# Linear attention beside a SwiGLU block on one core: a new order of work for the first five tiles

## The chip, the core and the metric

The kernel runs on one core of a Trainium2 chip. The core has five engines that work side by side and wait for each other through semaphores: TensorE (PE) multiplies matrices and writes to PSUM, ScalarE (ACT) evaluates functions, VectorE (DVE) does elementwise work and statistics, GpSimd (POOL) does elementwise work on SBUF, SyncE (SP) issues most DMAs. ACT issues some DMAs too. Every engine works its own queue strictly in the order in which it was written.

The metric is the device time of one execution in microseconds. The kernel before takes 211.72 us (median of three runs, 211.69 to 211.87). One further execution was profiled; it took 211.6 us, of which the profile's span covers 210.4.

## What is computed

The input x has 2048 rows of 512 in bfloat16. The output is the sum of three terms:

```python
xn = layernorm(x)                      # over the 512 columns, no scale or bias
q, k, v = xn @ wqkv                    # 32 heads of 16
phi = lambda t: where(t > 0, t + 1, exp(t)) + 1e-6
kv  = einsum("bhsd,bhse->bhde", phi(k), v)
z   = einsum("bhsd->bhd", phi(k))
o   = (phi(q) @ kv) / (phi(q) @ z + 1e-6)
out = x + o @ wo + (silu(x_ @ w_gate) * (x_ @ w_up)) @ w_down     # x_ is xn
```

The feature phi is built in the kernel as max(t, 0) + (min(exp(t), 1) + 1e-6).

## The kernel before

The 2048 rows are 16 tiles of 128. The kernel has two stages. In the first, for each tile, K and Q are projected (eight matmuls of 512 columns), phi(k) is formed, and the product of the normalized tile and phi(k) is accumulated over all tiles (`gtacc`, four matmuls, called GT below; it lives in the PSUM banks 4 to 7). In the second stage the SwiGLU block runs over four chunks of 512 rows, and the attention output and the projection back are added to it. The change lies in the first stage, and in its first five tiles above all.

No planner orders the work. The order is written out by hand: each call of a helper appends to the queue of one engine through `K.op(engine, function, r=reads, w=writes)`. `_Prog` keeps the last writer and the readers of each named resource and derives from them which semaphores an operation waits for. So the place of a call decides only its place in the queue of its own engine; the waits follow from the resources.

The steps that the change touches, with their engine and line:

- `bns` and `agg` (DVE, L296, L299): mean and variance of a tile. `rstd_pow` (L313): adds 1e-5 to the variance (L317, on POOL, for tiles 3 and 5 on DVE) and takes the power -0.5 (L324, always POOL).
- `xn_dve` (DVE, L304): the normalized tile, needs `rstd`. `xn(t)` is the same followed, from tile 3 on, by a DMA transpose on SP's queue (L377) that K and Q of the tile wait for.
- Tiles 0 to 2 take a shorter way: `xc_half` (DVE, L349) subtracts the mean, `tp_first` transposes on PE (L361) and copies on ACT (L370), `proj_first` (PE, L400) multiplies two of the four blocks of 128, and `rstd` is applied when ACT reads the result: `first_ek` (L457, exp of K), `first_pk` (L463, positive part of K), `first_eq` (L469, exp of Q), `first_pq` (L475, copy of Q).
- phi(k) of tile 0 is added on POOL (`feat_pool`, L482), of tiles 1 and 2 on DVE (`first_feat`, L489), after `clip` (DVE, L440) has cut the exponential.
- From tile 3 on: `kproj`, `qproj` (PE, L386), `exp_k` (ACT, L423), `exp_q` (ACT, L429 and the copy L433), `feat_k` (DVE: `clip` L440, `maxadd` L449, with the `zsum` of an earlier tile between them).
- `zsum` (POOL, L508 for tile 0, L512): adds phi(k) of a tile to the sum z. It is given the buffer of an exponential as a further read, so that it waits for the `clip` of a later tile.
- `fill` (PE, L268): matmuls on constants before the first data.

PSUM banks 0 to 3 hold K and Q of two tiles in turn: K of an even tile is in bank 0, Q in 1, K of an odd tile in 2, Q in 3. A projection thus waits until the readers of two tiles before are done. The loop over the tiles runs from tile 4. In step t it issues the projections and exponentials of tile t, the normalization of later tiles (`XN0`), the features of t, statistics of later tiles (`STAT`), and GT of tile t - 1 (from step 12 on of t - 2).

The queue of PE around the change runs: K 0, K 1, first halves of Q 0 and Q 1, second halves, K 2, GT 0, Q 2, GT 1, GT 2, K 3, Q 3, K 4, Q 4, GT 3, K 5, Q 5, GT 4 and so on. The queue of POOL runs: rstd 0 to 2, `feat_pool(0)`, rstd 3 to 7, zsum 0, rstd 8, zsum 1, rstd 9, zsum 2, rstd 10 and so on.

Of the kernel before, what the change touches and what calls it, by code (L numbers as in the profile page):

```python
# [6 lines left out]
ACT = mybir.ActivationFunctionType  # L7
# [101 lines left out]
def bass_parallel_sum__linear_attn_block__swiglu_ffn__prompt_kernel(  # L109
# [16 lines left out]
    with contextlib.ExitStack() as es:  # L126
# [120 lines left out]
        xload("sp", sp, 1, 1)  # L247
        wqkv_load("sp", sp, "wk", 1, 2, 1)
        wqkv_load("act", act, "wk", 1, 3, 1)
# [61 lines left out]
        VD = (3, 5)  # L311

        def rstd_pow(t):  # L313
            eng, h = ("dve", dve) if t in VD else ("pool", pool)
            K.op(
                eng,
                lambda: h.tensor_scalar(  # L317
                    out=vpe[:, t:t + 1], in0=mv[:, t, 1:2], scalar1=1e-5, scalar2=None, op0=ALU.add,
                ),
                r=[("mv", t)], w=[("vpe", t)],  # L320
            )
            K.op(
                "pool",
                lambda: pool.tensor_tensor(out=rstd[:, t:t + 1], in0=vpe[:, t:t + 1], in1=nhalf[:, :], op=ALU.pow),  # L324
                r=[("vpe", t), ("nhalf",)], w=[("rstd", t)],
            )
# [100 lines left out]
        def exp_q(t):  # L427
            K.op(
                "act", lambda: act.activation(eq[:, t, :], banks[qb(t)], ACT.Exp),  # L429
                r=[bk(qb(t))], w=[("eq", t)],  # L430
            )
            K.op(
                "act", lambda: act.activation(pkq[:, t, 1, :], banks[qb(t)], ACT.Copy),  # L433
                r=[bk(qb(t))], w=[("pq", t)],
            )
# [31 lines left out]
        def first_eq(t):  # L467
            K.op(
                "act", lambda: act.activation(eq[:, t, :], banks[qb(t)], ACT.Exp, scale=rstd[:, t:t + 1]),  # L469
                r=[bk(qb(t)), ("rstd", t)], w=[("eq", t)],  # L470
            )
# [20 lines left out]

        def feat_k(t):
            e = t % NE
            clip(ek[:, e, :], ("ek", e))
            if t >= 3:
                zsum(t - 3, e)
            maxadd(pkq[:, t, 0, :], banks[kb(t)], ek[:, e, :], [bk(kb(t)), ("ek", e)], [("pk", t)])
# [30 lines left out]
        def stat(t):  # L529
            bns(t)  # L530
            agg(t)
            rstd_pow(t)
# [6 lines left out]
        bns(0)  # L539
        agg(0)  # L540
        rstd_pow(0)
        xc_half(0, 0)
        xc_half(0, 1)
        bns(1)
        agg(1)
        rstd_pow(1)
        xc_half(1, 0)
        xc_half(1, 1)
        bns(2)
        agg(2)  # L550
        rstd_pow(2)
        xn_dve(0)
        xc_half(2, 0)
        xc_half(2, 1)

        fill(8, 512)
        tp_first(0, 0, 4)
        fill(2, P)
        tp_first(0, 1, 5)
        fill(3, P)  # L560
        proj_first(0, "wk", 0)
        tp_first(1, 0, 6)
        tp_first(1, 1, 7)
        proj_first(0, "wk", 1)
        first_ek(0)
        first_pk(0)
        proj_first(1, "wk", 0)
        proj_first(1, "wk", 1)
        first_ek(1)
        proj_first(0, "wq", 0)  # L570
        proj_first(1, "wq", 0)
        tp_first(2, 0, 4)
        tp_first(2, 1, 5)
        proj_first(0, "wq", 1)
        proj_first(1, "wq", 1)
        clip(ek[:, 0, :], ("ek", 0))
        feat_pool(0)
        bns(3)
        agg(3)
        rstd_pow(3)  # L580
        bns(4)
        clip(ek[:, 1, :], ("ek", 1))
        first_pk(1)
        first_eq(0)
        first_pq(0)
        proj_first(2, "wk", 0)
        proj_first(2, "wk", 1)
        gtacc(0)
        xn_dve(2)
        xn(3)  # L590
        agg(4)
        first_feat(1)
        rstd_pow(4)
        xn_dve(1)
        first_ek(2)
        first_pk(2)
        first_eq(1)
        first_pq(1)
        clip(ek[:, 2, :], ("ek", 2))
        xn(4)  # L600
        proj_first(2, "wq", 0)
        proj_first(2, "wq", 1)
        gtacc(1)
        first_eq(2)
        xload("act", act, 14, 2)
        first_pq(2)
        first_feat(2)
        bns(5)
        agg(5)
        rstd_pow(5)  # L610
        gtacc(2)
        bns(6)
        agg(6)
        rstd_pow(6)
        xn(5)
# [3 lines left out]
        exp_q(3)  # L619
        bns(7)  # L620
        clip(ek[:, 0, :], ("ek", 0))
        xn(6)
        agg(7)
        rstd_pow(7)
        zsum(0, 0)
        maxadd(pkq[:, 3, 0, :], banks[kb(3)], ek[:, 0, :], [bk(kb(3)), ("ek", 0)], [("pk", 3)])
        bns(8)
        xn(7)
        agg(8)
        rstd_pow(8)  # L630

        STAT = {4: (9,), 5: (10,), 6: (11,), 7: (12,), 8: (13, 14), 9: (15,)}
        XN0 = {5: (8,), 6: (9,), 7: (10,), 8: (11,), 9: (12, 13), 10: (14,)}
        XN1 = {}
        XN = {10: (15,)}

        for t in range(4, NT):
# [3 lines left out]
            exp_q(t)  # L641
            for i in XN0.get(t, ()):
                xn(i)
            feat_k(t)
            for i in XN1.get(t, ()):
                xn(i)
            for i in STAT.get(t, ()):
                stat(i)
            for i in XN.get(t, ()):
                xn(i)  # L650
            if t in (7, 8, 9):
                transpose_dma(t - 7)
            if t == 10:
                whalf("wg", wg_sb, B_w_gate, 0)
                whalf("wu", wu_sb, B_w_up, 0)
                wqkv_load("sp", sp, "wv", 2, 0, 4)
                wload("sp", sp, "wo", wo_sb, A_wo)
                whalf("wg", wg_sb, B_w_gate, 1)
            if t == 12:
                masks()  # L660
# [302 lines left out]
```

## Time and profile before

| what | before |
|---|---|
| median of three runs | 211.72 us |
| the profiled execution | 211.6 us, span 210.4 us |
| PE busy | 206.2 us, 98% |
| DVE busy | 119.8 us, 57% |
| ACT busy | 69.8 us, 33% |
| POOL busy | 74.5 us, 35% |
| DVE busy from 20 to 30 us | 8.94 of 10 us |
| POOL busy from 20 to 30 us | 8.92 of 10 us |
| granted TensorE clock | 1.00 |

The span counts from the first to the last instruction of the profiled execution; the difference to its time is what lies around it. Busy shares are means over the whole span, while the first stage, up to 48 us, loads DVE and POOL far more than the second. Matmuls overlap, and their ends are modelled, so the distance between the starts of two matmuls, 0.216 us for 512 columns, says more than the duration of one.

### The profile page before, as it was taken

Reading aid. Unit: us, or ns where it says so; the run is one execution under the profiler, and the core shown is the slowest. Engines: PE = TensorE matmul, PEld = TensorE weight load, DVE = VectorE, ACT = ScalarE, POOL = GpSimd, SP = SyncE. Lnnn points to the kernel's source line nnn. Section 1 sums busy time; section 2 is a strip of 40 time slices with the busy share of each in tenths; the row PEclk is TensorE's granted clock in tenths of the full one; section 3 lists DMA queues with packets and bytes.
Section 4 is the critical chain, followed back from the end, with each engine's and each line's share of the span. In section 5 each row is a group of like instructions: output and inputs, shape, how many; then the busy total and the mean of one; then the engine's idle time right before and its main releaser. Section 6 shows DMA issues by size and latency. Waiting matters only on the chain.

```text
span 210.4 us, 2758 instructions
## 1 busy us (share of the span) xinstructions
PE 206.2 (98%) x972; PEld 94.8 (45%) x991; DVE 119.8 (57%) x245; ACT 69.8 (33%) x122; POOL 74.5 (35%) x95
## 2 busy tenths in 40 slices
PE   8999999999999999999999999999999999999996
PEld 3444444445444444444444444444444444444444
DVE  3999989335365774547274746364556535374122
ACT  4887666666543331203122312212032213121000
POOL 3647987658032444222140432230414032221200
DMA  6853345794693011110202110202021010110201
GB/s 197 290 161 78 52 99 101 224 371 167 202 355 60 1 28 27 44 25 28 50 2 50 24 29 25 50 0 50 3 50 25 25 25 30 40 36 25 51 25 53
DMA packets 29455, 16.71 MB, mean 79 GB/s; under 512 B 20352, under 2 KB 29056, under 8 KB 29440
## 3 DMA queue, kind: packets, MB, share of 16 engines
q1 hardware_dynamic: 28304, 15.34, 26.7%
q10 hardware_dynamic: 1136, 1.18, 1.8%
q8 instruction: 8, 0.13, 0.3%
q14 instruction: 7, 0.06, 0.1%
HBM read 9.70 MB, written 2.10 MB: 56 GB/s over the span
## 4 chain that ended last, share of the span: by engine, by line
PE 93%; DMA 2%; POOL 2%; issue 1%; DVE 1%; ACT 1%; SPq 0%; DVEq 0%
PE psum L683 46%; PE psum L866 23%; PE psum L386 11%; PE psum L855 7%; PE psum L520 6%; DMA x_sb<-in_A_x_dram 2%; POOL rstd L324 1%; POOL pkq L482 1%; PE psum L781 0%; PE psum L804 0%; DVE stats L296 0%; DVE pkq L489 0%; ACT kpos L463 0%; ACT xcT L370 0%; POOL vpe L317 0%
## 5 line engine op out<-in xcount | busy, mean ns | idle before, releaser
L698 ACT ACTIVATE sg<-psum 128x512 bf16<-128x512 f32 x56 | 33.4, 598 | 106.8 <-PE psum L683 104.9
L683 PE MATMUL psum<-xnT,wu_sb 128*128 128x512 bf16 x222 | 57.4, 379 | 0.1
L683 PE MATMUL psum<-xnT,wg_sb 128*128 128x512 bf16 x217 | 56.0, 379 | 0.4
L813 POOL TENSOR_TENSOR prod<-pkq,zb 128x512 f32<-128x512 bf16 x16 | 18.6, 1161 | 57.8 <-DVE pkq L449 57.8
L683 PEld LDWEIGHTS psum<-xnT,wu_sb 128*128 128x128 bf16 x224 | 21.9, 98 | 26.4
L683 PEld LDWEIGHTS psum<-xnT,wg_sb 128*128 128x128 bf16 x224 | 21.9, 98 | 26.2
L879 DVE TENSOR_TENSOR out_sb<-psum,x_sb 128x512 bf16<-128x512 f32 (+2 forms) x17 | 11.2, 660 | 35.5 <-PE psum L866 35.5
L837 POOL TENSOR_TENSOR pqn<-pkq,rden 128x512 bf16<-128x512 bf16 x16 | 16.9, 1055 | 36.5 <-DVE rden L831 36.5
L704 DVE TENSOR_TENSOR pkq<-psum,sg 128x512 bf16<-128x512 f32 x28 | 19.1, 687 | 18.5 <-PE psum L683 14.0
L704 DVE TENSOR_TENSOR xn_sb<-psum,sg 128x512 bf16<-128x512 f32 x28 | 18.8, 671 | 14.5 <-PE psum L683 13.0
L866 PE MATMUL psum<-wd_sb,xn_sb 128*128 128x512 bf16 (+2 forms) x124 | 25.6, 355 | 0.1
L866 PE MATMUL psum<-wd_sb,pkq 128*128 128x512 bf16 x110 | 25.4, 379 | 0.1
L386 PE MATMUL psum<-wqkv_sb,xnT 128*128 128x512 bf16 x102 | 24.1, 379 | 0.1
L512 POOL TENSOR_TENSOR zacc<-zacc,pkq 128x512 f32<-128x512 f32 x15 | 17.3, 1154 | 5.0 <-DVE ek L440 4.6
L866 PEld LDWEIGHTS psum<-wd_sb,xn_sb 128*128 128x128 bf16 x126 | 11.8, 98 | 12.5
L866 PEld LDWEIGHTS psum<-wd_sb,pkq 128*128 128x128 bf16 x112 | 11.0, 98 | 13.2
L855 PE MATMUL psum<-m_sb,eq 128*128 128x512 bf16 (+2 forms) x66 | 16.2, 366 | 0.1
L520 PE MATMUL psum<-pkq,xn_sb 128*128 128x512 bf16 x63 | 15.9, 379 | 0.2
L386 PEld LDWEIGHTS psum<-wqkv_sb,xnT 128*128 128x128 bf16 x104 | 10.2, 98 | 12.3 <-DMA xnT<-xn_sb 0.3
L821 DVE TENSOR_REDUCE den<-prod 128x32 f32<-128x512 f32 x16 | 10.9, 684 | 5.9 <-POOL prod L813 5.9
L296 DVE BATCH_NORM_STATS2 stats<-x_sb 128x6 f32<-128x512 bf16 x16 | 10.9, 683 | 3.1 <-DMA x_sb<-in_A_x_dram 3.1
L449 DVE SCALAR_TENSOR_TENSOR pkq<-pkq,eq 128x512 bf16<-128x512 bf16 x16 | 11.1, 692 | 0.6
(59 smaller groups left out, 137.6 us busy)
## 6 DMA issues: line engine op xcount, KB each, us to landing
out_dram<-out_sb SPq DMA_DIRECT2D x15, 128.0 KB, 1.7
wg_sb<-in_B_w_gate_dram SPq DMA_DIRECT2D x2, 896.0 KB, 8.5
wu_sb<-in_B_w_up_dram SPq DMA_DIRECT2D x2, 896.0 KB, 6.1
wd_sb<-in_B_w_down_dram SPq DMA_DIRECT2D x1, 1792.0 KB, 9.9
x_sb<-in_A_x_dram SPq DMA_DIRECT2D x2, 512.0 KB, 4.1
x_sb<-in_A_x_dram SPq DMA_DIRECT2D x4, 128.0 KB, 3.8
wqkv_sb<-in_A_wqkv_dram SPq DMA_DIRECT2D x1, 512.0 KB, 9.5
wo_sb<-in_A_wo_dram SPq DMA_DIRECT2D x1, 512.0 KB, 10.3
```

What stands on the lines that cost most here:

```text
L386: (lambda c=c: pe.matmul(banks[b], xnT[:, c, t * P:(t + 1) * P], wqkv_sb[:, c, lo:lo + D], start=(c == 0), stop=(c == NDC - 1),))
L449: lambda: dve.scalar_tensor_tensor(out=dst, in0=src, scalar=0.0, in1=e, op0=ALU.max, op1=ALU.add,),
L512: lambda: pool.tensor_tensor(out=zacc[:, :], in0=zacc[:, :], in1=pk, op=ALU.add),
L520: (lambda c=c: pe.matmul(banks[4 + c], xn_sb[:, t, c * P:(c + 1) * P], pkq[:, t, 0, :], start=(t == 0), stop=(t == NT - 1),))
L683: (lambda c=c: pe.matmul(banks[b], w_sb[:, c, fc * P:(fc + 1) * P], xnT[:, c, C * 512:(C + 1) * 512], start=(c == 0), stop=(c == NDC - 1),))
L698: lambda: act.activation(sg[:, j % NSG, :], banks[gb], ACT.Silu),
L704: lambda: dve.tensor_tensor(out=hT(C, fc), in0=banks[ub], in1=sg[:, j % NSG, :], op=ALU.mult,),
L813: lambda: pool.tensor_tensor(out=p, in0=pkq[:, t, 1, :], in1=zb[:, :], op=ALU.mult),
L837: lambda: pool.tensor_tensor(out=pqn[:, t % NPN, :].rearrange("p (h e) -> p h e", e=DH), in0=pkq[:, t, 1, :].rearrange("p (h e) -> p h e", ...
L855: (lambda g=g: pe.matmul(dst, pqnT(t)[:, g, :], m_sb[:, g, lo:hi], start=(g == 0), stop=False,))
L866: (lambda fc=fc: pe.matmul(dst, hT(C, fc)[:, jj * P:(jj + 1) * P], wd_sb[:, fc, lo:hi], start=False, stop=(fc == NFC - 1),))
L879: lambda: dve.tensor_tensor(out=o, in0=src, in1=x_sb[:, t, lo:hi], op=ALU.add),
```

## The change

- The exponentials of Q of tiles 0 to 2 no longer read PSUM with the scale `rstd`. `first_eq` goes, and `late_eq` on ACT reads the copy of Q in bfloat16 (already scaled) in the steps 11, 12 and 13 of the loop. The copy `copy_q` is now a helper of its own, called right behind `exp_q` everywhere.
- The load of x 14 and 15 on ACT's queue moves from between the exponential and the copy of Q 2 to step 5 of the loop.
- The order of tiles 0 to 4 is written anew. On PE, GT 0 comes behind Q 2, and K 3 and Q 3 come ahead of GT 2; GT 3 stays behind Q 4. On DVE, xn 0 goes ahead of `bns(2)`, both clips of tiles 0 and 1 stand together, xn 1 and xn 3 come ahead of `bns(4)`, and `maxadd` of tile 4 ahead of xn 7. On POOL, `feat_pool(0)` stands behind rstd 3 instead of ahead of it, and zsum 0 and zsum 1 behind rstd 9, without the wait for a later clip.
- Step 4 leaves the loop and is written out; the statistics of tile 9 are issued before the loop.
- Two loads of blocks of wk change places in the program text, which lie on different queues. The fillers of 128 columns are split 3 and 2 instead of 2 and 3.

```diff
--- before.py
+++ after.py
@@ -245,8 +245,8 @@
         xload("sp", sp, 0, 1)
         wqkv_load("act", act, "wk", 1, 0, 2)
         xload("sp", sp, 1, 1)
+        wqkv_load("act", act, "wk", 1, 3, 1)
         wqkv_load("sp", sp, "wk", 1, 2, 1)
-        wqkv_load("act", act, "wk", 1, 3, 1)
         xload("act", act, 2, 1)
         wqkv_load("sp", sp, "wq", 0, 0, 1)
         wqkv_load("act", act, "wq", 0, 1, 1)
@@ -308,10 +308,8 @@
                 r=[("x", t), ("mv", t), ("rstd", t)], w=[("xn", t)],
             )
 
-        VD = (3, 5)
-
-        def rstd_pow(t):
-            eng, h = ("dve", dve) if t in VD else ("pool", pool)
+        def eps(t, eng):
+            h = dve if eng == "dve" else pool
             K.op(
                 eng,
                 lambda: h.tensor_scalar(
@@ -319,6 +317,8 @@
                 ),
                 r=[("mv", t)], w=[("vpe", t)],
             )
+
+        def rstd_of(t):
             K.op(
                 "pool",
                 lambda: pool.tensor_tensor(out=rstd[:, t:t + 1], in0=vpe[:, t:t + 1], in1=nhalf[:, :], op=ALU.pow),
@@ -429,6 +429,8 @@
                 "act", lambda: act.activation(eq[:, t, :], banks[qb(t)], ACT.Exp),
                 r=[bk(qb(t))], w=[("eq", t)],
             )
+
+        def copy_q(t):
             K.op(
                 "act", lambda: act.activation(pkq[:, t, 1, :], banks[qb(t)], ACT.Copy),
                 r=[bk(qb(t))], w=[("pq", t)],
@@ -464,10 +466,10 @@
                 r=[bk(kb(t)), ("rstd", t)], w=[("kpos", t)],
             )
 
-        def first_eq(t):
-            K.op(
-                "act", lambda: act.activation(eq[:, t, :], banks[qb(t)], ACT.Exp, scale=rstd[:, t:t + 1]),
-                r=[bk(qb(t)), ("rstd", t)], w=[("eq", t)],
+        def late_eq(t):
+            K.op(
+                "act", lambda: act.activation(eq[:, t, :], pkq[:, t, 1, :], ACT.Exp),
+                r=[("pq", t)], w=[("eq", t)],
             )
 
         def first_pq(t):
@@ -490,12 +492,17 @@
                 r=[("kpos", t), ("ek", t)], w=[("pk", t)],
             )
 
+        def clip_k(t):
+            clip(ek[:, t % NE, :], ("ek", t % NE))
+
+        def maxadd_k(t):
+            e = t % NE
+            maxadd(pkq[:, t, 0, :], banks[kb(t)], ek[:, e, :], [bk(kb(t)), ("ek", e)], [("pk", t)])
+
         def feat_k(t):
-            e = t % NE
-            clip(ek[:, e, :], ("ek", e))
-            if t >= 3:
-                zsum(t - 3, e)
-            maxadd(pkq[:, t, 0, :], banks[kb(t)], ek[:, e, :], [bk(kb(t)), ("ek", e)], [("pk", t)])
+            clip_k(t)
+            zsum(t - 3, t % NE)
+            maxadd_k(t)
 
         def feat_q(t):
             clip(eq[:, t, :], ("eq", t))
@@ -529,7 +536,8 @@
         def stat(t):
             bns(t)
             agg(t)
-            rstd_pow(t)
+            eps(t, "pool")
+            rstd_of(t)
 
         def xn(t):
             xn_dve(t)
@@ -537,117 +545,130 @@
                 transpose_dma(t)
 
         bns(0)
+        fill(8, 512)
         agg(0)
-        rstd_pow(0)
         xc_half(0, 0)
         xc_half(0, 1)
+        tp_first(0, 0, 4)
+        fill(3, P)
+        tp_first(0, 1, 5)
+        fill(2, P)
+        eps(0, "pool")
+        rstd_of(0)
+        proj_first(0, "wk", 0)
         bns(1)
         agg(1)
-        rstd_pow(1)
         xc_half(1, 0)
+        tp_first(1, 0, 6)
+        eps(1, "pool")
         xc_half(1, 1)
-        bns(2)
-        agg(2)
-        rstd_pow(2)
-        xn_dve(0)
-        xc_half(2, 0)
-        xc_half(2, 1)
-
-        fill(8, 512)
-        tp_first(0, 0, 4)
-        fill(2, P)
-        tp_first(0, 1, 5)
-        fill(3, P)
-        proj_first(0, "wk", 0)
-        tp_first(1, 0, 6)
         tp_first(1, 1, 7)
+        rstd_of(1)
         proj_first(0, "wk", 1)
+        first_pk(0)
         first_ek(0)
-        first_pk(0)
         proj_first(1, "wk", 0)
         proj_first(1, "wk", 1)
         first_ek(1)
+        xn_dve(0)
         proj_first(0, "wq", 0)
         proj_first(1, "wq", 0)
+        bns(2)
+        agg(2)
+        xc_half(2, 1)
+        xc_half(2, 0)
         tp_first(2, 0, 4)
+        eps(2, "pool")
         tp_first(2, 1, 5)
-        proj_first(0, "wq", 1)
-        proj_first(1, "wq", 1)
-        clip(ek[:, 0, :], ("ek", 0))
-        feat_pool(0)
+        rstd_of(2)
         bns(3)
         agg(3)
-        rstd_pow(3)
+        eps(3, "dve")
+        rstd_of(3)
+        proj_first(0, "wq", 1)
+        clip_k(0)
+        clip_k(1)
+        xn_dve(1)
+        xn_dve(3)
         bns(4)
-        clip(ek[:, 1, :], ("ek", 1))
+        agg(4)
+        first_pq(0)
         first_pk(1)
-        first_eq(0)
-        first_pq(0)
+        first_feat(1)
+        proj_first(1, "wq", 1)
+        first_pq(1)
         proj_first(2, "wk", 0)
         proj_first(2, "wk", 1)
-        gtacc(0)
-        xn_dve(2)
-        xn(3)
-        agg(4)
-        first_feat(1)
-        rstd_pow(4)
-        xn_dve(1)
         first_ek(2)
         first_pk(2)
-        first_eq(1)
-        first_pq(1)
-        clip(ek[:, 2, :], ("ek", 2))
-        xn(4)
         proj_first(2, "wq", 0)
         proj_first(2, "wq", 1)
+        first_pq(2)
+        feat_pool(0)
+        gtacc(0)
         gtacc(1)
-        first_eq(2)
-        xload("act", act, 14, 2)
-        first_pq(2)
-        first_feat(2)
-        bns(5)
-        agg(5)
-        rstd_pow(5)
-        gtacc(2)
-        bns(6)
-        agg(6)
-        rstd_pow(6)
-        xn(5)
+        transpose_dma(3)
         kproj(3)
         exp_k(3)
         qproj(3)
         exp_q(3)
+        copy_q(3)
+        xn_dve(2)
+        eps(4, "pool")
+        rstd_of(4)
+        xn(4)
+        bns(5)
+        agg(5)
+        clip_k(2)
+        eps(5, "dve")
+        first_feat(2)
+        gtacc(2)
+        rstd_of(5)
+        xn(5)
+        stat(6)
+        clip_k(3)
+        maxadd_k(3)
+        kproj(4)
+        exp_k(4)
+        xn(6)
         bns(7)
-        clip(ek[:, 0, :], ("ek", 0))
-        xn(6)
+        qproj(4)
+        exp_q(4)
+        copy_q(4)
+        clip_k(4)
         agg(7)
-        rstd_pow(7)
-        zsum(0, 0)
-        maxadd(pkq[:, 3, 0, :], banks[kb(3)], ek[:, 0, :], [bk(kb(3)), ("ek", 0)], [("pk", 3)])
+        eps(7, "pool")
         bns(8)
+        maxadd_k(4)
+        rstd_of(7)
         xn(7)
         agg(8)
-        rstd_pow(8)
-
-        STAT = {4: (9,), 5: (10,), 6: (11,), 7: (12,), 8: (13, 14), 9: (15,)}
+        eps(8, "pool")
+        rstd_of(8)
+        stat(9)
+        gtacc(3)
+        zsum(0, None)
+        zsum(1, None)
+
+        STAT = {5: (10,), 6: (11,), 7: (12,), 8: (13, 14), 9: (15,)}
         XN0 = {5: (8,), 6: (9,), 7: (10,), 8: (11,), 9: (12, 13), 10: (14,)}
-        XN1 = {}
         XN = {10: (15,)}
 
-        for t in range(4, NT):
+        for t in range(5, NT):
             kproj(t)
             exp_k(t)
             qproj(t)
             exp_q(t)
+            copy_q(t)
             for i in XN0.get(t, ()):
                 xn(i)
             feat_k(t)
-            for i in XN1.get(t, ()):
-                xn(i)
             for i in STAT.get(t, ()):
                 stat(i)
             for i in XN.get(t, ()):
                 xn(i)
+            if t == 5:
+                xload("act", act, 14, 2)
             if t in (7, 8, 9):
                 transpose_dma(t - 7)
             if t == 10:
@@ -656,6 +677,8 @@
                 wqkv_load("sp", sp, "wv", 2, 0, 4)
                 wload("sp", sp, "wo", wo_sb, A_wo)
                 whalf("wg", wg_sb, B_w_gate, 1)
+            if t in (11, 12, 13):
+                late_eq(t - 11)
             if t == 12:
                 masks()
             if t >= 12:
```

## The prediction

> **What bounds the kernel now.** I read the page first (busy shares, chain by line), then the chain in order of time, then the timelines of PE, DVE, POOL and ACT from 0 to 48 us, and last the landings of the transposing DMAs.
>
> The page: 98% of the span is TensorE. Only an idle stretch of PE can be won, and a new one is paid for in full.
>
> ```profile
> span 210.4 us, 2758 instructions
> PE 206.2 (98%) x972; PEld 94.8 (45%) x991; DVE 119.8 (57%) x245; ACT 69.8 (33%) x122; POOL 74.5 (35%) x95
> ```
>
> The chain in order of time (start, us, what) shows where PE last waited for anyone: for the features of tile 2 (`first_feat(2)`, L489), just before the four matmuls of GT 2. From 13.16 on it is PE alone to 208.54, with gaps of 0.05.
>
> ```profile
> 12.42 0.69 DVE pkq L489
> 13.12 0.05 issue
> 13.16 1.04 PE psum L520 x4
> 14.20 3.45 PE psum L386 x16
> 17.65 0.86 PE psum L520 x4
> ```
>
> One matmul of 512 columns is 3.45 / 16 = 0.216, so four are 0.86 and eight 1.73. GT 1 starts at 12.02 (PE's timeline) and ends at 12.88; GT 2 starts at 13.16. That gap, 0.28, is all the idle time after 6.16; the earlier gaps (5.39 to 5.84 for xc 1) belong to steps whose order on every queue stays. So **the gain is at most 0.28 us, 0.13%**.
>
> The timelines of DVE and POOL carry the rest. DVE is busy 8.94 of the 10 us from 20 to 30, POOL 8.92, and they hold each other up:
>
> ```profile
> 33.65 0.57 POOL L324 TENSOR_TENSOR rstd<-vpe,nhalf 128x1 f32<-128x1 f32 x1
> 34.19 1.16 POOL L512 TENSOR_TENSOR zacc<-zacc,pkq 128x512 f32<-128x512 f32 x1
> ```
>
> ```profile
> 24.60 0.43 DVE L304 TENSOR_SCALAR xn_sb<-x_sb,mv,rstd 128x512 bf16<-128x512 bf16 x1
> ...
> 32.95 0.38 DVE L304 TENSOR_SCALAR xn_sb<-x_sb,mv,rstd 128x512 bf16<-128x512 bf16 x1
> ...
> 34.26 1.24 DVE L304 TENSOR_SCALAR xn_sb<-x_sb,mv,rstd 128x512 bf16<-128x512 bf16 x1
> ```
>
> An `xn` takes 0.38 alone (32.95). That of tile 15 was released by POOL's `rstd` (ends 34.22); POOL had gone straight on to a `zsum` at 34.19, and the `xn` took 1.24: it ended 0.15 after the `zsum` (35.34). The one at 24.60 also ended 0.15 after a `zsum` (23.73 + 1.15). A wide POOL operation that starts first holds an `xn` to its end. In the kernel before only tile 15, with nothing urgent behind it, pays this in full.
>
> The landings: the transpose of tile 3 is issued at 10.45 and lands 2.5 later; that of tile 4 at 12.5, 3.1 later, beside the load of x 14 and 15 (issued 12.22); later ones take 2.4.
>
> **What the change does at no cost.** On the ACT queue the exponentials of Q 0 to 2 go (0.70, 0.73, 0.75). The last copy of Q 2 came at 13.75 and comes at 12.04 at the earliest. No PE step waited for ACT there but Q 2 (0.3 before its weight load at 11.10), so this alone wins nothing more. Three exponentials come back at t = 11 to 13. No row has one that reads SBUF; the nearest are 0.59 (L433) and 0.75 (L469), below nothing is excluded as they are added work. I take 0.60. ACT idles 0.69 before each K exponential there (39.32, 41.91, 44.50), so they cost 0; at 0.75 the K exponential would come 0.06 late, and DVE idles 1.5 beside it. The load of x 14 and 15 (0.33 on ACT's queue) moves some 7 us later; its first reader, `bns(14)`, ran at 29.6, landing takes 2.9, so 0, and tile 4's transpose should land in 2.4. The two wk loads swap places between different queues: no queue changes, 0. The 13 fillers are cut 8+3+2 instead of 8+2+3: the second transposes start one filler (0.06) later, and their output is needed at 6.16: 0. The swapped halves of xc 2 are done by 7.6, needed at 8.34: 0. xn 0 before `bns(2)` moves DVE by 0.29, counted below.
>
> **Step one, xn 3.** DVE, start to start by rows: bns 0.72 with its agg behind it, agg 0.21 to its dependent and 0.10 to another, xc half 0.20, clip 0.21, xn 0.30, first_feat 0.57, maxadd 0.58. From 5.90: xn 0, bns 2 6.19, agg 2 6.91, xc 7.12 and 7.32, bns 3 7.52, agg 3 8.24, eps 3 8.45, clips 8.52 and 8.73, xn 1 8.94 to 9.33. POOL: rstd 3 from 8.68, ends with DVE's run at 9.37 (the rstd at 9.25 also took 0.72 beside clip and xn, ending 0.04 after them). POOL's next is now `feat_pool(0)`, L482, moved from before rstd 3 to behind it: 1.15, from 9.33 to 10.48. xn 3 waits for the same rstd 3 and starts at 9.41, second, so it ends near 10.63, as tile 15's did, against 10.42 before. Its bounds are 9.8 (not held) and 10.65; I take the held one, as the same pair of releases is there in the trace. The transpose is issued at 10.66 and lands at 13.16 (13.06 to 13.76 by 2.4 to 3.1).
>
> PE now has no GT 2 in front of K 3: GT 0 11.15, GT 1 12.09 (first_feat 1 on DVE 11.37 to 12.03), ready for K 3 at 12.95. It waits until about 13.2. The wait on features has become a wait on a transpose, and the 0.28 is gone: GT 3 would follow at 13.2 + 20 x 0.216 = 17.52, against 17.49.
>
> **Step two, DVE falls behind.** From xn 3's end the queue is bns 4 10.55, agg 4 11.27, first_feat 1 11.37, xn 2 11.94, then a wait for rstd 4: eps 4 is held behind first_feat as before (10.60 took 0.57), to 12.10, rstd 4 to 12.75, xn 4 12.85; transposed 13.26, landed 15.66. bns 5 13.15, clip 2 13.97, first_feat 2 14.27 to 14.95: GT 2 15.0 (ready 14.93). K 4 15.87, GT 3 17.60. xn 5 15.07, bns 6 15.38, maxadd 3 16.51, xn 6 17.39 behind rstd 6, bns 7 17.71, bns 8 18.62, maxadd 4 19.22, xn 7 19.81, bns 9 20.21, agg 9 20.93. Before, agg 9 was at 20.02: 0.9 later. PE is meanwhile only 0.11 late: GT 4 20.19, GT 5 22.78 (pk 5 ready 22.7).
>
> **Step three, POOL's sums.** zsum 0 and 1 ran at 17.64 and 19.41, between the statistics; now both stand behind rstd 9. rstd 8 ends 21.27, rstd 9 22.62, zsum 0 22.58, zsum 1 23.16 to 24.31 (rows 0.61, 1.15). xn 9 reaches it at 23.38, held to 24.46; clip 6 24.38 and maxadd 6 24.70 follow, GT 6 starts 25.45. zsum 2 gets in behind clip 6, 24.67 to 25.8, eps 10 and rstd 10 (0.35 + 0.57) end at 26.67, against 23.77. DVE is at xn 10 by 26.1 and waits 0.6; then zsum 3 is first again: xn 10 runs 26.7 to 27.94, clip 7 27.86, maxadd 7 28.20 to 28.90. GT 7, which PE could start at 28.04, starts at **28.95, against 27.85: 1.1 late**. One tile on, zsum 4 holds xn 11 to 30.1, which GT 8 (31.54) covers. xn 13 waits for rstd 13, two statistics late in t = 8, runs 33.05, maxadd 9 33.7 to 34.4: GT 9 at **34.45, against 30.44 + 2.59 = 33.03: 1.42 late**. After t = 10 there are no statistics; GT 10 comes only behind K 12, Q 12, and POOL idled 0.6 to 1.4 per tile there, so the backlog drains (xn 15 held once more, needed by K 15 some 8 us later). The weight loads behind xn 15's transpose slip by as much as PE.
>
> **Sum.** 1.4 us on the profiled execution's own 211.6 (span 210.4 and 1.2 around it) is 213.0; the median, 211.72, is 0.1 above that execution.
>
> **A rule against a row.** The pow of rstd 14 at 30.96 began inside xn 13 (30.87 to 31.29), a clip followed to 31.49, and it ended at 31.53 after its usual 0.57: small POOL operations are held for their last part only. If instead they waited out the whole run of DVE and then took 0.55, rstd 3 would end near 9.9 and all that follows be 0.5 later: 213.5. The Trainium skill, SBUF — State Buffer, section Who interferes with whom, says that whichever of a two-port DVE operation and a GpSimd one issues first has the shared ports for the whole instruction and the other is fully blocked. By that rule the sum would be the 213.5; by the row it stays 213.0.
>
> **The rivals.** (1) The backlog alone: xn 3 isn't held, as POOL takes `feat_pool(0)` up late. Then xn 3 ends at 9.8, K 3 starts at 12.88, agg 9 comes at 20.1, rstd 9 ends at 21.75, rstd 10 near 25.7. xn 10 is held to 27.1, GT 7 starts at 28.05 (0.2 late) and GT 9, for xn 13 behind rstd 13, near 33.5 to 33.65 (0.5 to 0.6): 212.1. For it: only start times 0.08 apart decide; against it: the pair at 34.19 and 34.26. (2) Not slower: the sums fill POOL's waits. The place is rstd 10; if it ends by 25.3 with no zsum behind it that holds xn 10, pk 7 is there by 27.57 and PE keeps its 0.28: 211.3. POOL's idle time between 15 and 19 (0.28, 0.70, 0.33) speaks for room, its 8.92 of 10 us from 20 to 30 against it. (3) The holding by whole instructions, above: 213.5, up to 214.
>
> **How the numbers follow.** What a measurement here can tell from no change is about 0.2%, 0.42 us. My forecast, 212.5 to 213.4, has 0.50; rival 1 (211.8 to 212.4) 0.20, of which 0.08 within 0.42; rival 2 0.21, of which 0.04 for more than the 0.28 that I can see; rival 3 0.09. Faster 0.04, same 0.17 + 0.08 = 0.25, slower 0.71. The range 211.3 to 213.6 leaves out part of rival 3 and the unseen gain, and takes in both bounds of xn 3.
>
> **What would show it.** xn 3 near 1.2 us and ending 0.15 after POOL's L482; a PEld wait on the transpose at K 3 near 13 us; zsum 0 after 22; xn 10 waiting for rstd, then long; PE waits on L449 before GT 7 and GT 9. If the `xn` rows are 0.4 each, step one is wrong; if PE is solid from 13 to 35, step three is, and the time is 211.3.

## The result, and the profile after

The changed kernel takes 213.09 us (median of 7 runs, 212.63 to 214.28) beside 211.84 (7 runs, 211.69 to 212.28): a ratio of 1.0061, 95% interval 1.0045 to 1.0078. It is slower, by more than the 0.2% that can be told. 213.0 was forecast.

The profiled execution took 214.28, the slowest of the seven; its span is 212.9, against 210.4 before. The granted clock is 1.00 in both. The first lines of the page of the changed kernel (busy us, share of the span, instructions):

```profile
span 212.9 us, 2778 instructions
PE 208.3 (98%) x991; PEld 95.1 (45%) x991; DVE 121.5 (57%) x245; ACT 69.6 (33%) x122; POOL 74.4 (35%) x95
```

The work is the same and the shares are too (the trace of before lacks 19 of the 991 matmuls, so PE's two busy times can't be compared); PE's waits must be found one by one. In the changed kernel the helpers stand some lines lower: GT is L527, `feat_pool` L484, `first_feat` L491, `maxadd` L451, `clip` L442, eps L315, `zsum` L515 and L519; L304, L324, L377 and L386 are as before. Tile 3 of x landed at 8.0 in this execution instead of 7.1, so its first half is some 0.5 late throughout.

The chain of the changed kernel in order of time (start, us, what):

```profile
9.19 0.70 POOL rstd L324
9.89 0.03 issue
9.92 1.09 DVE xn_sb L304
...
14.82 1.07 POOL rstd L324
15.89 0.02 issue
15.91 0.41 DVE xn_sb L304
...
20.53 0.40 DVE xn_sb L304
20.93 0.03 DVE mv L299
20.96 4.98 DMA xnT<-xn_sb
25.94 0.14 issue
26.07 1.89 PE psum L386 x8
```

Before, the chain is PE alone from 13.16 on. Now it runs through DVE and POOL to 20.93, and then waits for a DMA: the transpose of tile 7 is issued at 20.96 and lands 4.98 later, where the same transpose took 2.4 before. K 7 starts at 26.07 after a wait of 1.63; PE is solid from there on, so this late landing, not the features, sets this execution's end. GT 9 starts at 35.57, against 33.03: 2.54 of the 2.68 by which the two profiled executions differ. Of these 2.54, 0.64 was there at K 6 already (21.58 against 20.94), most of it from the late x 3.

The backlog that the prediction worked out is there as well. DVE's and POOL's timelines of the changed kernel (start, us, engine, line, operation, what its engine waited for):

```profile
26.89 1.23 DVE L304 TENSOR_SCALAR xn_sb<-x_sb,mv,rstd 128x512 bf16<-128x512 bf16 x1 [0.35 <-POOL rstd L324]
```

```profile
9.70 1.16 POOL L484 TENSOR_TENSOR pkq<-kpos,ek 128x512 bf16<-128x512 f32 x1
...
26.29 0.57 POOL L324 TENSOR_TENSOR rstd<-vpe,nhalf 128x1 f32<-128x1 f32 x1
26.82 1.16 POOL L519 TENSOR_TENSOR zacc<-zacc,pkq 128x512 f32<-128x512 f32 x1
```

xn 3 ends at 11.01, 0.15 after `feat_pool(0)` (9.70 + 1.16): held, as forecast. xn 10 waits 0.35 for rstd 10, then takes 1.23 and ends 0.14 after a `zsum` (26.82 + 1.16): held too.

### The profile page after: what moved, and what is told of

Same layout as the page of the kernel before. It is cut to its first block, busy times and chain, and to the rows that moved or that the text cites. A ratio compares the mean times of both kernels' runs of the same rounds, so it can differ in the third digit from the quotient of the medians.

```text
span 212.9 us, 2778 instructions
## 1 busy us (share of the span) xinstructions
PE 208.3 (98%) x991; PEld 95.1 (45%) x991; DVE 121.5 (57%) x245; ACT 69.6 (33%) x122; POOL 74.4 (35%) x95
## 4 chain that ended last, share of the span: by engine, by line
PE 87%; DMA 5%; DVE 4%; POOL 2%; SPq 1%; issue 1%; DVEq 0%
PE psum L706 45%; PE psum L889 23%; PE psum L386 7%; PE psum L878 6%; PE psum L527 4%; DMA x_sb<-in_A_x_dram 3%; DMA xnT<-xn_sb 2%; DVE stats L296 2%; POOL rstd L324 1%; DVE xn_sb L304 1%; DVE mv L299 0%; PE psum L804 0%; PE psum L827 0%; SPq L209 0%; POOL vpe L315 0%
## 5 line engine op out<-in xcount | busy, mean ns | idle before, releaser
L706 PE MATMUL psum<-xnT,wg_sb 128*128 128x512 bf16 x224 | 57.5, 379 | 0.0
L706 PEld LDWEIGHTS psum<-xnT,wg_sb 128*128 128x128 bf16 x224 | 21.9, 98 | 26.2
L386 PE MATMUL psum<-wqkv_sb,xnT 128*128 128x512 bf16 x104 | 24.4, 379 | 1.8 <-DMA xnT<-xn_sb 1.8
L519 POOL TENSOR_TENSOR zacc<-zacc,pkq 128x512 f32<-128x512 f32 x15 | 17.4, 1160 | 5.1 <-DVE ek L442 4.6
L889 PEld LDWEIGHTS psum<-wd_sb,pkq 128*128 128x128 bf16 x112 | 10.9, 98 | 13.2
L386 PEld LDWEIGHTS psum<-wqkv_sb,xnT 128*128 128x128 bf16 x104 | 10.0, 97 | 14.6 <-issue 2.3
L527 PE MATMUL psum<-pkq,xn_sb 128*128 128x512 bf16 x64 | 16.1, 379 | 0.1
L451 DVE SCALAR_TENSOR_TENSOR pkq<-pkq,eq 128x512 bf16<-128x512 bf16 x16 | 11.1, 692 | 0.6
```

The source lines that it names most:

```text
L386: (lambda c=c: pe.matmul(banks[b], xnT[:, c, t * P:(t + 1) * P], wqkv_sb[:, c, lo:lo + D], start=(c == 0), stop=(c == NDC - 1),))
L519: lambda: pool.tensor_tensor(out=zacc[:, :], in0=zacc[:, :], in1=pk, op=ALU.add),
L527: (lambda c=c: pe.matmul(banks[4 + c], xn_sb[:, t, c * P:(c + 1) * P], pkq[:, t, 0, :], start=(t == 0), stop=(t == NT - 1),))
L706: (lambda c=c: pe.matmul(banks[b], w_sb[:, c, fc * P:(fc + 1) * P], xnT[:, c, C * 512:(C + 1) * 512], start=(c == 0), stop=(c == NDC - 1),))
L889: (lambda fc=fc: pe.matmul(dst, hT(C, fc)[:, jj * P:(jj + 1) * P], wd_sb[:, fc, lo:hi], start=False, stop=(fc == NFC - 1),))
```

## The experiments

The theories, by the letters used below. **A**, the prediction's: DVE falls 0.9 behind, POOL's sums hold back rstd 10 and xn 10, and the features for GT 7 and GT 9 come late. **B**: the load of x 14 and 15, issued at 20.93 right beside the transpose of tile 7, delays its landing. **C**, formed after the first four runs: with DVE 0.9 late, transposes 6 and 7 are issued so late that PE has no slack left for a landing of 4 to 5 us, which comes in either kernel. **D**, in three expectations: DVE's lateness alone is the bound, whatever POOL's sums do. (The first expectations call the late transpose tile 8's; it is tile 7's.)

**The changed kernel again**, on the chip of the next three.

> The changed kernel once more, for a second profile. Theory A (POOL's long additions hold DVE: xn 3 behind feat_pool(0), xn 10 behind zsum 3, and rstd 10 and 13 late because zsum 0 and 1 stand behind rstd 9): 213.1 us (212.6 to 213.4), xn 3 about 1.1 and xn 10 about 1.2 us long, and even where no transpose is late PE waits for DVE's L451 before GT 7 or GT 9, GT 9 1.2 to 1.8 us later than the 33.03 of the kernel before. Theory B (the moved load of x 14 and 15 meets the transpose of tile 8, as the first profile of the changed kernel shows: issued at 20.93 and 20.96, landed 4.5 and 5.0 us later): the transpose of tile 8 lands over 4 us after its issue again, and K 8 waits for it by 1 us or more.

Measured: 213.13 (212.65 to 214.25, 6 runs) beside 211.96 (11 runs); 1.0058, interval 1.0036 to 1.0080. Its profiled execution took 213.25. The chain of this run:

```profile
18.04 0.03 DVE stats L296
18.07 4.39 DMA xnT<-xn_sb
22.47 0.14 issue
22.60 1.89 PE psum L386 x8
```

Now the late landing is tile 6's: issued 18.07, landed 4.39 later, K 6 at 22.60 against 20.94, 1.66 late, and that is the whole of 213.25 - 211.6. The load of x 14 was issued only at 20.42: B can't explain this one. maxadd 9 ran from 33.31 to 34.00 and GT 9 started at 34.69, so A's lateness is hidden behind this one. xn 3 took 1.09 and ended 0.14 after `feat_pool(0)`, as A expects. xn 10 was not held (0.54), a miss: K 6 being late, `clip` 6 came late too and was the one that a sum held (1.24 instead of 0.29).

**The load of x 14 and 15 back** between the positive part of K 2 and the copy of Q 2 on ACT's queue.

```diff
         first_pk(2)
+        xload("act", act, 14, 2)
         proj_first(2, "wq", 0)
...
-            if t == 5:
-                xload("act", act, 14, 2)
```

> The changed kernel with the load of x 14 and 15 back between the positive part of K 2 and the copy of Q 2 on ACT's queue. Theory A: 212.7 to 213.2, no less than 0.9 us over the kernel before, since POOL and DVE are untouched; the transpose of tile 4 may take 3.1 instead of 2.4. Theory B: the transpose of tile 8 lands in 2.4, K 8 no longer waits, and the time falls to 211.4 to 212.0.

Measured: 212.78 (212.71 to 212.87, 5 runs); 1.0039, interval 1.0025 to 1.0054. In the profiled execution no transpose behind T3 landed late, and the 5 runs lie within 0.16. The load is issued at 10.43, beside T3 (12.22 and beside T4 in the kernel before); T3 lands after 3.27, so K 3 starts at 13.91. The chain of this run:

```profile
10.51 3.27 DMA xnT<-xn_sb
...
24.30 1.20 POOL zacc L519
25.51 0.20 POOL vpe L315
25.70 0.07 issue
25.78 0.57 POOL rstd L324
26.35 1.13 POOL zacc L519
...
33.34 0.70 DVE pkq L451
34.04 0.05 issue
34.09 1.04 PE psum L527 x4
```

This is A without late landings of T6 and T7. POOL goes from sum to rstd 10 to sum, maxadd 9 ends at 34.03, and GT 9 starts at 34.09, 1.06 after the 33.03 of before. K 3's delay is swallowed by it, though it is not small: by PE's own work GT 9 could have started at 33.80 (K 9 at 32.07, and 1.73), 0.77 late without A. That no T6 or T7 was late looked like B, whose load was gone; later runs overturn that.

**Sums 0 and 1 back among the statistics**, behind rstd 7 and rstd 8.

```diff
         rstd_of(7)
+        zsum(0, None)
...
         rstd_of(8)
+        zsum(1, None)
...
-        zsum(0, None)
-        zsum(1, None)
```

> The changed kernel with zsum 0 back behind rstd 7 and zsum 1 behind rstd 8. Theory A: rstd 10 comes 1.5 us or more sooner, xn 10 does not wait for it, GT 9 no later than 0.6 over the kernel before: 212.0 to 212.5. Theory B: the transpose of tile 8 is as late as before, 212.9 to 213.2.

Measured: 213.82 (212.96 to 214.48, 6 runs); 1.0085, interval 1.0064 to 1.0105: the slowest of all, and a miss for A. rstd 10 does come 2.0 sooner (24.28), but DVE, still 0.9 late, now meets zsum 1 at xn 8 (DVE's and POOL's timelines of this run):

```profile
22.16 1.23 DVE L304 TENSOR_SCALAR xn_sb<-x_sb,mv,rstd 128x512 bf16<-128x512 bf16 x1 [0.21 <-POOL rstd L324]
```

```profile
22.09 1.15 POOL L519 TENSOR_TENSOR zacc<-zacc,pkq 128x512 f32<-128x512 f32 x1
```

The hold has moved from xn 10 to xn 8, and T6 landed late again (4.01; K 6 waited 0.99). Where the sums stand decides which tile is hit. The hold also delays T8, to 23.42 (22.09 in the changed kernel run again): PE, without a late T6, would need it 3.3 later, where it has 4.2 in that run. That may be why this version is the slowest; the one trace doesn't show it.

**`feat_pool(0)` also waits for xn 3**, so that it can't hold it.

```diff
-                r=[("kpos", t), ("ek", t)], w=[("pk", t)],
+                r=[("kpos", t), ("ek", t), ("xn", 3)], w=[("pk", t)],
```

> The changed kernel with feat_pool(0) on POOL waiting also for xn 3, so that xn 3 is not held. Theory A: xn 3 takes 0.4 instead of 1.1, its transpose is issued 0.7 sooner, K 3 does not wait, DVE's queue runs 0.7 sooner to tile 9; the backlog of the sums stays: 212.0 to 212.5. Theory B: only the 0.2 us at K 3 goes, 212.8 to 213.1.

Measured: 212.96 (212.65 to 213.44, 6 runs); 1.0050, interval 1.0034 to 1.0066. DVE's and POOL's timelines of this run:

```profile
9.21 0.89 DVE L304 TENSOR_SCALAR xn_sb<-x_sb,mv,rstd 128x512 bf16<-128x512 bf16 x2
...
10.84 1.11 DVE L491 TENSOR_TENSOR pkq<-kpos,ek 128x512 bf16<-128x512 f32 x1
```

```profile
10.25 1.16 POOL L484 TENSOR_TENSOR pkq<-kpos,ek 128x512 bf16<-128x512 f32 x1 [0.60 <-DVE xn_sb L304]
```

xn 1 and xn 3 now take 0.89 together instead of 1.57, and K 3 doesn't wait. But `feat_pool(0)`, later by that much, holds `first_feat(1)` instead: 1.11 instead of 0.66. The next instruction on DVE, xn 2, starts at 11.88, against 11.81 in the changed kernel run again: nothing is won, and A's 212.0 to 212.5 is missed. GT 9 starts at 34.16, again behind maxadd 9. The Trainium skill, SBUF — State Buffer, section Who interferes with whom, says that a DVE instruction with two SBUF inputs contends with a GpSimd instruction that reads SBUF; `first_feat` is one, and the 1.11 agrees.

**Every sum two tiles later**, five of them behind the loop.

```diff
-            zsum(t - 3, t % NE)
+            zsum(t - 5, t % NE)
...
-        zsum(0, None)
-        zsum(1, None)
...
+        zsum(NT - 5, None)
+        zsum(NT - 4, None)
```

> The changed kernel with every zsum two steps later: zsum 0 in step 5 behind clip 5, zsum 1 in step 6 and so on, five of them behind the loop instead of three. POOL's additions are the same, but none stands between rstd 9 and zsum 2's old place. Theory A (POOL's solid run of sums and statistics from rstd 9 to rstd 13 sets xn 13, and with it maxadd 9 and GT 9): rstd 13 some 1.7 us sooner, xn 10 no longer waits, GT 9 is no longer waited for; the time falls to 211.7 to 212.1 where no transpose is late. Theory C (the transposes of tiles 6 to 9 have only 3.1 to 3.4 us from their issue to their projection, and one that meets a fetch of instructions lands 4 to 5 us after its issue): the scatter stays, single runs 1 us or more above the lowest. Theory D (DVE alone, late by 0.9 us since xn 3, is the bound): 212.6 or more still.

Measured: 213.07 (212.36 to 213.94, 6 runs); 1.0063, interval 1.0042 to 1.0084. xn 10 no longer waits for rstd 10 and isn't held (25.66, 0.50), but PE's timeline of this run shows a transpose late in its place (T7, 4.84 after issue):

```profile
25.45 1.89 PE L386 MATMUL psum<-wqkv_sb,xnT 128*128 128x512 bf16 x8 [1.48 <-DMA xnT<-xn_sb]
```

With PE late, maxadd 9 comes no sooner (33.44), so this trace can't say whether GT 9 is free of A. The lowest run, 212.36, is above A's 212.1.

**All three suspects undone at once**: the sums two tiles later, `feat_pool(0)` waiting for xn 3, and the load of x 14 and 15 among the first loads, behind that of x 5.

```diff
+        xload("act", act, 14, 2)
...
-                r=[("kpos", t), ("ek", t)], w=[("pk", t)],
+                r=[("kpos", t), ("ek", t), ("xn", 3)], w=[("pk", t)],
...
-            zsum(t - 3, t % NE)
+            zsum(t - 5, t % NE)
...
-            if t == 5:
-                xload("act", act, 14, 2)
...
```

> The changed kernel with three things: the sums two steps later, feat_pool(0) waiting for xn 3, and the load of x 14 and 15 on ACT's queue right behind that of x 5. Theory A: K 3 unstalled, GT 9 not waited for: 211.4 to 211.8, no worse than the kernel before. Theory C: the same with less scatter, if the load of x 14 and 15 takes part in the late landings. Theory D: 212.4 or more.

Measured: 212.49 (212.09 to 213.54, 10 runs); 1.0041, interval 1.0026 to 1.0055. Still slower, though for a reason of its own: the early load delays x 3 (there at 8.54 instead of 7.04 in the changed kernel run again) and the weights, K 3 starts at 14.12 instead of 13.2, and PE, dense from there, reaches GT 9 at 34.12 (K 10 at 32.39, and 1.73). This run says little on A or C.

**The sums alone, in the kernel before**: zsum 0 and 1 behind rstd 9.

```diff
-        zsum(0, 0)
...
-            if t >= 3:
+            if t >= 5:
...
+            if t == 4:
+                zsum(0, None)
+                zsum(1, None)
```

> The kernel before with one part alone: zsum 0 and zsum 1 behind rstd 9, without the wait for a later clip. Theory A: POOL's backlog comes as in the changed kernel, but starts 0.9 us sooner, since DVE is not late: rstd 10 near 25.5, xn 10 held, GT 9 0 to 0.6 late: 211.8 to 212.4. Theory C: no scatter, as the transposes are issued as before. Theory D: 211.8.

Measured: 211.87 (211.38 to 212.49, 12 runs) beside 211.90 (27 runs); 1.0002, interval 0.9991 to 1.0013. DVE's timeline of this run shows the same hold of xn 10, and it costs nothing:

```profile
24.87 1.24 DVE L304 TENSOR_SCALAR xn_sb<-x_sb,mv,rstd 128x512 bf16<-128x512 bf16 x1 [0.23 <-POOL rstd L324]
```

It is at 24.87 here and at 26.38 to 27.05 where the change is in and the sums stand behind rstd 9: the DVE queue isn't 0.9 behind here, and PE doesn't notice.

**The load of x 14 and 15 alone, in the kernel before**, moved to step 5.

```diff
-        xload("act", act, 14, 2)
...
+            if t == 5:
+                xload("act", act, 14, 2)
```

> The kernel before with one part alone: the load of x 14 and 15 in step 5. Theory A: no change, 211.6 to 211.9. Theory C: a transpose near it may land 3 to 5 us after its issue, but K 6 to K 9 come 4.3 to 5.8 us after the issue there, so at most 0.5 us in a single run: 211.6 to 212.0. Were the moved load by itself the cause: 212.3 or more.

Measured: 211.81 (211.57 to 212.40, 12 runs); 0.9998, interval 0.9985 to 1.0010. The line of the transposes (L377) in this run, for that of tile 8 alone (issued at 21.02), from issue to landing:

```profile
DMA to landing us min/median/max: 5.0/5.0/5.0
```

A late landing in the order of the kernel before, and no one waits: it is there at 26.06, K 8 starts at 26.40. This fits C; the load (20.56 to 23.29) runs beside this transpose.

**The load of x 14 and 15 in step 6**, in the changed kernel.

```diff
-            if t == 5:
+            if t == 6:
```

> The changed kernel with the load of x 14 and 15 one step later, in step 6, about 2.6 us later, when the transposes under way are those of tiles 8 and 9. (Of the runs so far: the transpose that waits in the first profile of the changed kernel is that of tile 7, and K 7 waits for it; the expectations written before named tile 8.) Theory A (POOL's solid run sets GT 9): nothing falls below 212.6. Theory C (a fetch of instructions of 16 KB that begins 1.2 us or more after a transpose was issued makes it land 4 to 5 us after its issue, and tiles 6 and 7 have only 3.0 to 3.3 us from issue to projection): the scatter of 212.6 to 214.3 stays, since the fetch stays. If the load of x 14 and 15 is what makes tile 7 late: all runs between 212.6 and 212.9.

Measured: 213.29 (212.66 to 213.49, 6 runs) beside 211.73 (23 runs); 1.0053, interval 1.0034 to 1.0072. T6 landed after 4.29 and K 6 waited 1.26, while the load was issued only at 24.52 (PE's timeline of this run, K 6):

```profile
22.59 1.89 PE L386 MATMUL psum<-wqkv_sb,xnT 128*128 128x512 bf16 x8 [1.26 <-DMA xnT<-xn_sb]
```

So a landing of over 4 us needs no load: B falls as the cause of them all. A share is left to it: beside the load in step 5 alone, T7 landed after 3.5 in the run in which `feat_pool` waits, and K 7 started at 24.11, 0.26 after PE was ready (22.98 + 0.87); A's floor hid that. In step 6 the load stands beside T9 (4.25), which has the cover.

**The sums two tiles later, and the load in step 6**: A taken away, C left.

> The changed kernel with both: the sums two steps later, and the load of x 14 and 15 in step 6. Theory A and C: GT 9 is no longer waited for, so the lowest runs are 212.2 to 212.4 (K 3, GT 2 and the like still 0.3 to 0.5 late), single runs up to 1.5 us above them for a late transpose. If the load of x 14 and 15 makes tile 7 late: all runs within 212.1 to 212.5.

Measured: 212.84 (211.91 to 213.67, 12 runs); 1.0043, interval 1.0025 to 1.0061. The two lowest are 211.91 and 211.94, 0.7 below anything that the changed kernel reached in 13 runs (212.63) and below the run before this one, on the same chip, with the load alone moved (212.66). So the floor of A has gone, and with it D, which put a bound at 212.6; the median stays where C puts it. PE's timeline of this run, K 7 and K 8:

```profile
24.86 1.89 PE L386 MATMUL psum<-wqkv_sb,xnT 128*128 128x512 bf16 x8 [0.71 <-DMA xnT<-xn_sb]
...
27.81 1.89 PE L386 MATMUL psum<-wqkv_sb,xnT 128*128 128x512 bf16 x8 [0.20 <-DMA xnT<-xn_sb]
```

**PE's new order and the load alone, in the kernel before**: K 3 and Q 3 ahead of GT 2, DVE's and POOL's queues untouched.

```diff
-        gtacc(2)
...
         exp_q(3)
+        gtacc(2)
...
+            if t == 5:
+                xload("act", act, 14, 2)
```

> The kernel before with what is left of the change where POOL and DVE are not touched: GT 2 behind Q 3 on PE, and the load of x 14 and 15 in step 5. K 3 then waits for its transpose (landed 12.98) instead of GT 2 for its features (13.16), and tile 4's transpose lands 0.7 us sooner. Theory A: a gain of 0.1 to 0.15 us, 211.5 to 211.8 beside a kernel before of 211.7 to 211.9, hardly to be told from none. If K 4 waits for its transpose: no gain, 211.7 to 212.0.

Measured: 211.72 (211.39 to 212.16, 12 runs) beside 211.73; 0.9993, interval 0.9980 to 1.0006. K 3 waits 0.24 for T3 in place of the 0.28 of GT 2, and GT 9 starts at 33.10. T8 landed after 4.66, covered. The new order on PE wins nothing that can be told, and costs nothing.

**Less cover alone, in the kernel before**: transposes 6 and 7 also wait for xn 7 and xn 8.

```diff
-        def transpose_dma(t):
+        def transpose_dma(t, after=()):
...
-                r=[("xn", t)], w=[("xnT", t)],
+                r=[("xn", t)] + list(after), w=[("xnT", t)],
...
-            if t >= 3:
+            if t in (7, 8):
+                transpose_dma(t - 1, [("xn", t)])
+            if t >= 3 and t not in (6, 7):
```

> The kernel before with only the transposes of tiles 6 and 7 issued later: that of tile 6 waits also for xn 7, that of tile 7 also for xn 8. They are then issued near 18.4 and 20.75 instead of 16.66 and 18.42, and land 2.4 us later where nothing is in their way, at 20.8 and 23.2, just ahead of K 6 (20.94) and K 7 (23.53); POOL, DVE and ACT run as before. Theory C (the fetch of 16 KB of instructions, which comes between 19 and 27 us, meets a transpose; what changed is that tiles 6 and 7 lost their cover): lowest runs as the kernel before, 211.4 to 211.7, single runs 1 us or more above, median 212.1 to 212.8. Theory A alone (the holds of DVE by POOL are all there is, the late landings are accidents of the changed kernel): 211.6 to 212.0, like the kernel before.

Measured: 212.58 (211.55 to 214.05, 11 runs) beside 211.80 (16 runs); 1.0047, interval 1.0021 to 1.0074. Three runs are at 213.9 to 214.05, where the kernel before never went above 212.7 in all its runs. T6 is issued 2.54 ahead of K 6 there and T7 2.81 ahead of K 7, somewhat less cover than the changed kernel has; T8, behind T7 in the queue, has 4.2 instead of 5.4. Its profiled execution, at 212.58, shows no late landing for these two tiles (a first load was late, and GT 2 started at 14.04): that the high runs are those with a late T6 or T7 is read from their size and from the runs above, not seen in this trace.

**Where the late landings come from.** Each trace has one packet of 16 KB on an instruction queue between 19 and 28 us, 1.0 to 1.6 us long. The DMA view of the changed kernel run again, from 19.3 to 20.8 (packets, MB, share of 16 engines):

```profile
q8 instruction: 1, 0.02, 6.7%
```

All 14 profiles, ordered by when that packet began, counted from the issue of the transpose that it met (in brackets the transpose behind it, where that was late too; "no" also where the load was issued only when the transpose would usually have landed, or later):

| kernel | transpose | packet after issue | landing after issue | load of x 14 and 15 beside it | PE waited |
|---|---|---|---|---|---|
| x 14 back | 9 | -0.07 | 2.65 | no | 0 |
| before | 8 | -0.05 | 2.70 | no | 0 |
| sums alone | 8 | 0.14 | 2.98 | no | 0 |
| sums later, load in step 6 | 7 (8) | 1.01 | 4.07 (5.51) | no (yes) | 0.71 (0.20) |
| changed | 7 (8) | 1.23 | 4.98 (4.79) | yes | 1.63 (0) |
| load in step 6 | 6 | 1.30 | 4.29 | no | 1.26 |
| changed, again | 6 | 1.30 | 4.39 | no | 1.36 |
| sums back | 6 | 1.32 | 4.01 | no | 0.99 |
| sums later | 7 (8) | 1.34 | 4.84 (4.66) | yes | 1.48 (0) |
| `feat_pool` waits | 9 | 1.91 | 4.40 | no | 0 |
| all undone | 9 | 1.95 | 4.33 | no | 0 |
| less cover | 10 | 1.99 | 4.12 | no | 0 |
| PE's order | 8 | 2.56 | 4.66 | yes | 0 |
| load alone | 8 | 2.98 | 5.03 | yes | 0 |

With the packet alone the late landings are 4.0 to 4.4, with the load as well 4.7 to 5.0 (5.5 in a bracket): so B adds some 0.6, an estimate from these rows. The other transposes take 2.4 to 2.6 for the most part and 3.0 to 3.5 beside that load. A packet of 8 KB on a second instruction queue, between 23.8 and 26.2 in each trace, matters less: beside it a transpose took 2.9 to 3.4 in four traces, and 3.9 and 4.2 where the load came too.

The packets show what happens. A transpose is 512 packets of 256 bytes and 32 of 4. In the run with the load in step 6, T6's packets begin from 19.34 on, none begins from 20.2 to 20.8, and the last 43 begin from 20.82 to 21.64; the 16 KB packet ends at 20.84. All packets of T5, in the same run, begin within 0.9 us. In the three other traces with a late T6 or T7 and no load beside it, 41 to 43 packets likewise begin only as the 16 KB packet ends, and in the run in which `feat_pool` waits the last two (27.60, against 27.62). In the first three rows the transpose ahead had all its packets out by then, and landed as usual. So the rest of a transpose can stand behind an instruction fetch. In the last two rows only one or two packets were left when the fetch began, later than the transpose usually lands: there the load had made it late first.

The Trainium skill, Runtime: NRT & Kernel Launch, section Instruction fetch mechanics, says that an engine's instructions are refilled in blocks of 16 KiB by DMA while it runs, at a cost that is mostly hidden. The size agrees with the packet here; that the cost is hidden does not hold here for a transpose with less than some 4 to 5 us of cover. No run moved the fetch, and why it begins anywhere from 19.4 to 27.9 stays open.

What a late landing costs is a matter of cover, from the issue to the projection. Two rows of SP's timeline of the kernel before, T6 and T7, and two of PE's, K 6 and K 7:

```profile
16.66 1.19 SPq L377 DMA_TRANSPOSE xnT<-xn_sb  x1
...
18.42 1.19 SPq L377 DMA_TRANSPOSE xnT<-xn_sb  x1
```

```profile
20.94 1.89 PE L386 MATMUL psum<-wqkv_sb,xnT 128*128 128x512 bf16 x7
...
23.53 1.89 PE L386 MATMUL psum<-wqkv_sb,xnT 128*128 128x512 bf16 x8
```

That is 4.3 and 5.1 of cover. In the changed kernel run again T6 is issued at 18.07 and T7 at 20.45, while PE would have been ready for K 6 near 21.1 and for K 7 near 23.7: 3.0 and 3.2.

## Why the prediction was right, and where not

The time was right (213.0, measured 213.09), and so was the sign, but only one of two causes was named; that the two together come out at the forecast is in part chance.

- **What bounds the kernel, and a gain of at most 0.28.** Right as far as tested: PE's order with the load moved gives 0.9993 (0.9980 to 1.0006).
- **The parts at no cost.** Right where tested: the load alone 0.9998. An exponential that reads SBUF takes 0.63 to 0.66, where 0.60 was taken, and nothing waits for it.
- **Step one, xn 3.** Right: held to 0.15 behind `feat_pool(0)`, its transpose issued at 10.5 in the changed kernel run again (forecast 10.66), 2.5 to land. K 3 waits 0.16.
- **Step two, DVE 0.9 late.** Right, if a little small: agg 9 at 21.12 (changed kernel again), forecast 20.93, before 20.02. What **failed** is "later ones take 2.4", said of the transposes' landings: it was read from one execution, in which T8 took 2.70, T9 2.91 and T15 3.19, and no cover was worked out from it. T6 and T7 lost 1.3 and 1.9 of theirs, and their landings of up to 4.4 and 5.0 then reached PE. This is the step that missed C.
- **Step three, the sums.** Right in kind, mis-sized by 0.36. With x 14 back, xn 10 ran 26.38 to 27.62 (forecast 26.7 to 27.94), maxadd 9 33.34 to 34.03 (33.7 to 34.4), GT 9 at 34.09 instead of 34.45: the term is 1.06, not 1.42. eps 9 was not held behind xn 8 and `clip` 5, so that rstd 9 ended at 22.34 instead of 22.62, and what is behind it moved up. GT 7 is at 28.61, not 28.95. And the sums are no cause by themselves (1.0002 alone): they cost only where DVE is late.
- **The sum.** A, and C, which the sum lacks, don't add up. Where A is seen without late T6 and T7 the median is 0.8 above that of before (x 14 back, where K 3 was late as well); C alone gives +0.8 (less cover) and +1.1 (sums later, load in step 6), both together 1.17 and 1.25. A late transpose sets PE back before GT 9, and A's wait then shrinks by as much. A sets a floor: the lowest runs of the changed kernel stand 0.94 and 1.12 above the lowest of before on the same chip. C lifts single executions above it, up to 214.28.
- **The rule against the row.** The row was taken for every small POOL operation, and that failed for one. rstd 3 took 0.69, as forecast, but rstd 5 took 1.06 (14.82 to 15.88) against its usual 0.57, behind `first_feat(2)` (14.78, 0.69, two SBUF inputs), and xn 5 waited 0.44. There waiting for the whole instruction fits better than the row. The Trainium skill, SBUF — State Buffer, section Who interferes with whom, states that for DVE operations in a two-port mode; of one with two SBUF inputs it says that it contends with a GpSimd instruction that reads SBUF, and the 1.06 agrees.
- **The rivals.** Rival 1 assumed that DVE is in time once xn 3 isn't held; the run in which `feat_pool` waits shows that `first_feat(1)` is held instead, with the same lateness behind it. Rival 2 needed rstd 10 by 25.3; it ended at 26.35. Rival 3 forecast 213.5 by a hold at rstd 3 which didn't come.

What stays open: why the 5 runs with x 14 back show no late landing at all. K 6 and K 7 stand 0.6 later there (cover 3.6 and 3.8), which is still less than 4.0 to 4.4; by the rows above such a landing would have put GT 9 some 0.2 to 0.6 behind this floor (an estimate), so it may be chance. Nor is it settled how often the fetch meets T6 or T7: of the changed kernel only two executions were profiled, and it did in both; and the run that takes the cover alone shows its price in the median, but no late landing in its one trace. No version here beats the kernel before.

## What to carry to other kernels

When an engine that isn't the bound falls behind, write down for each transfer that it issues how much time is left until its reader, and hold that against the slowest landing in any trace, not the usual one. Two late chains that end at the same engine give the later of the two, not their sum; undo one, and the other is still there. Moving an operation on POOL out of the way of one DVE instruction put it in the way of another here, twice (`feat_pool(0)`, and the sums 0 and 1); look for idle time on DVE first.

## What the runs showed of the hardware

- A DMA transpose of 128x512 mostly takes 2.4 to 2.6 us from issue to landing, and 3.0 to 3.5 beside a load of 256 KB. Where an instruction fetch of 16 KB began 1.0 to 2.0 us after its issue, it took 4.0 to 4.4, with the load as well 4.7 to 5.0; its last packets began as the fetch's packet ended. Where the fetch began with it, it took 2.65 to 2.98.
- A wide POOL operation that has started holds an `xn` (1.23 instead of 0.38), a `clip` (1.24 instead of 0.29) and an addition of two SBUF inputs on DVE (1.11 instead of 0.66) to its end; a power of 128x1 on POOL is held by such an addition (1.06 instead of 0.57), but not much by a run of `clip` and `xn` (0.69).
